# Attention of all batches with float32 operands in two column tiles

## The chip, the cores and the metric

The kernel runs on one core of a Trainium2 chip. The time is device microseconds of one execution; a run's time is compared as a median over several runs. One further execution is recorded by the hardware profiler, and the rows below come from it.

The engines' short names in the rows: PE is TensorE (matmuls), PEld its weight loads, DVE VectorE, ACT ScalarE, POOL GpSimd, SP SyncE, which here only issues DMA transfers. TensorE has two clock levels, 1.2 and 2.4 GHz, and the profile gives the granted clock of a stretch as a share of the higher.

## The reference

```python
def sm_attn(qq, kk, vv):                       # 8 batches, 8 heads
    s = scale * np.matmul(qq, kk.transpose(0, 1, 3, 2))
    a = np.exp(s - np.max(s, axis=-1, keepdims=True))
    return np.matmul(a / (np.sum(a, axis=-1, keepdims=True) + 1e-09), vv)
p_packed = sm_attn(p, k, v)                    # 32 packs; seq 576, head_dim 64
out = sm_attn(q, p_packed, p_packed)
x = out as 4608 tokens x 512
h = x @ w_in                                   # 512 -> 2048
x = (h * sigmoid(1.702 * h)) @ w_out           # 2048 -> 512
h = max(x @ w1, x @ w2, x @ w3)                # 512 -> 768
return h @ w_out2                              # 768 -> 512
```

## The kernel before, in words

The work of one batch is split into two groups of four heads; a group is written b_g, so 6_0 is batch 6, heads 0 to 3. One group's attention has these steps, which `steps()` lists with time numbers: `load_pk` (p and k), `split_pk`, `load_v`, `s1` (first scores, in two halves of 288 tokens) with `sm1`, `t1` and `t1r` (transposes of the exponentials, into `et`), `load_q`, `pv` (value products, with a mask product `pn` on VectorE), `pt` (transposes of the packed result, `ptp`), `s2` (second scores, in two halves), `sm2`, `sm3`, `tr2` (which end in `at`).

A float32 operand can go to TensorE in two ways. Where `mm3` (lines 102 to 106) is used, it is split into a high and a low fp32r part, and a product takes three matmuls (lines 104, 105, 106). Where a matmul is given float32 operands directly, it takes two passes, and each pass is a record in the trace. Batches under `NB = 4` take the second way in `s1`, `s2` and `pv`: the scores with 64 weight columns for each of two column tiles (the upper and lower half of the output's partitions, lines 297 and 401), the value product with 128 weight columns and 256 moving columns (line 358). Batches 4 to 7 take `mm3`, and split k, q, v, p and the transposed exponentials on ScalarE and VectorE (lines 127 to 133, 239 to 242). In both, the value product computes 256 columns of which the mask keeps a quarter, and GpSimd copies the packed results of two batches into shared tiles `sp` (line 393), from which `pw` is made (their product with `w_in`, 512 columns).

The gate block follows: `h` (from `at` and `pw`, 288 tokens at a time), tanh-based gating on ScalarE and VectorE (lines 542 to 550), `acc` (the out-projection). Then comes the block with the maximum of three products. All of its large matmuls, and those of the gate block, are `mm3`.

The order is not a loop's. `main()` adds each step with a time number to a plan, which is sorted; a scheduler then places the instructions on the engines by their waits and buffers, and pools hand the buffers out again once read. Attention of batches 0 and 1 fills the start; that of a later pair of batches is spread among the gate block's work on the pair before. The weights `w_in` and `w_out` are loaded in four quarters, each piece as a raw load (line 141) and a low load (line 149, what lies shifted by two bytes), from which VectorE makes the fp32r parts (lines 157 to 189). SyncE's queue issues these and the loads of p, k, v and q in program order, so that a load whose buffer is not free holds up those behind it. `keep_busy` (line 200) puts filler matmuls between the steps of the first groups.

Of the kernel before, what the change touches and what calls it, by code (L numbers as in the profile page):

```python
# [8 lines left out]
F32 = mybir.dt.float32  # L9
# [10 lines left out]
P = 128  # L20
# [8 lines left out]
NB = 4  # L29
# [15 lines left out]
def tile_packed_attention_moe(  # L45
# [42 lines left out]

    def ur_tile(name):
        return urp.tile([P, S], F32, tag="ur", name=name)  # L90
# [117 lines left out]
    class Group:  # L208
        def __init__(self, b, g):
            self.b, self.g, self.n = b, g, f"{b}_{g}"  # L210

        def load_pk(self):
            b, g = self.b, self.g
            self.praw = ap_.tile([P, 2, NP], F32, tag="praw", name=f"praw_{self.n}")
            nc.sync.dma_start(self.praw, p[b, g])
            self.kraw = self.load_t(k, "k")

        def split_pk(self):
            if self.b < NB:
                t = u_tile(f"pbd_{self.n}")  # L220
                nc.gpsimd.memset(t[:, :2 * P], 0.0)
                for x in range(2):
                    r = slice(D * x, D * x + D)
                    to = t[r, :384].rearrange("p (a b) -> p a b", b=192)[:, :, NP * x:NP * x + NP]
                    nc.vector.tensor_copy(to, self.praw[r])
                self.pbd = t
                return
            t = u_tile(f"pbd_{self.n}", F32R)
            nc.gpsimd.memset(f(t), 0.0)
            for x in range(2):  # L230
                r = slice(D * x, D * x + D)
                hi, lo = (
                    t[:, 192 * y:192 * y + 384].rearrange("p (a b) -> p a b", b=192)[
                        r, :, 96 * y + NP * x:96 * y + NP * x + NP
                    ]
                    for y in range(2)
                )
                eng = nc.gpsimd if 0 else nc.vector
                eng.tensor_copy(hi, self.praw[r])
                eng.tensor_tensor(out=lo, in0=self.praw[r], in1=f(hi), op=ALU.subtract)  # L240
            self.pbd = [t[:, HALF * y:HALF * y + 2 * P] for y in range(2)]
            self.k = self.split_t(self.kraw, "k")

        def load_t(self, src, name):
            raws = []
            for c in range(2):
                raws.append((u_tile if self.b < NB and name == "q" else ur_tile)(f"raw_{name}_{self.n}_{c}"))
                nc.sync.dma_start(raws[-1], src[self.b, 2 * self.g + c])
            return raws

        def split_t(self, raws, name):
            t = []
            for c in range(2):
                hl = [u_tile(f"{name}{x}_{self.n}_{c}", F32R) for x in range(2)]
                split(raws[c], *hl, self.b)
                t.append(hl)
            return t

        def load_v(self):
            self.vraw = []  # L260
            for c in range(3):
                raw = (u_tile if self.b < NB else ur_tile)(f"raw_v_{self.n}_{c}")
                if c < 2:
                    nc.sync.dma_start(raw[:, :TB], v[self.b, self.g, :, c])
                else:
# [823 lines left out]
```

## Time and profile before

| what | value |
| --- | --- |
| median of 3 runs | 1351.38 us (1349.59 to 1352.53) |
| profiled execution | 1349.93 us |
| its span, first to last instruction | 1348.2 us |
| TensorE busy | 1327.8 us, 98% |
| VectorE busy | 966.4 us, 72% |
| ScalarE busy | 566.2 us, 42% |
| GpSimd busy | 116.3 us, 9% |
| mean granted clock | 0.997 |

The records of matmuls overlap, since they are pipelined: one of 288 columns is shown with some 0.29 us, and the next starts earlier than that. What a matmul costs is therefore read from the distance between starts. A row such as "184.63 1.19 PE L401 MATMUL s<-raw_q,pbd 128*64 128x288 f32 x8" is eight records beginning at 184.63 us and ending 1.19 us later, line 401, output s from raw_q and pbd, weights of 128 x 64, 128 x 288 moving elements. A "<-" in brackets names what ended the idle time ahead of a row.

### The profile page before, as it was taken

How to read it: one execution, taken by the hardware profiler on the slowest of the kernel's cores; microseconds unless marked ns; L12 is line 12 of the kernel's file. 1: busy time of each engine (PE TensorE's matmuls, PEld its weight loads, DVE VectorE, ACT ScalarE, POOL GpSimd, SP SyncE). 2: the span in 40 equal slices, each digit the busy share in tenths (PEclk: the TensorE clock that was granted, in tenths of full speed). 3: DMA queues.
4: the chain of work that ended last, by engine and by line, in shares of the span. 5: the costliest groups of instructions: out<-in, count | busy, mean ns of one | idle time of the engine just before them, and what ended most of it. 6: DMA issues, size and time to landing. Idle time of an engine off the chain costs nothing.

```text
span 1348.2 us, 22369 instructions
## 1 busy us (share of the span) xinstructions
PE 1327.8 (98%) x8486; PEld 1255.4 (93%) x8486; DVE 966.4 (72%) x1984; ACT 566.2 (42%) x1188; POOL 116.3 (9%) x246
## 2 busy tenths in 40 slices
PE   6899999999999999999999999999999999999998
PEld 4699898999999999999999999999999899999997
DVE  6899976887767676859999988736645567366461
ACT  3566544665555555545656542222311312223111
POOL 1110000100000001000000001101001011010000
PEclk9999999999999999999999999999999999999999
DMA  8769634543233313216756629947647567475451
GB/s 325 270 241 390 241 101 129 177 118 129 71 107 115 93 44 120 91 47 213 234 182 203 217 89 362 332 152 271 235 172 246 191 223 266 152 268 192 166 186 47
DMA packets 91692, 249.71 MB, mean 185 GB/s; under 512 B 10944, under 2 KB 40128, under 8 KB 84672
## 3 DMA queue, kind: packets, MB, share of 16 engines
q0 software_dynamic: 24640, 132.66, 28.8%
q1 hardware_dynamic: 66944, 115.62, 25.4%
q8 instruction: 67, 1.10, 0.3%
q14 instruction: 41, 0.34, 0.1%
HBM read 204.47 MB, written 43.78 MB: 184 GB/s over the span
## 4 chain that ended last, share of the span: by engine, by line
PE 94%; DVE 4%; ACT 1%; issue 1%; DMA 0%; SPq 0%; POOL 0%; ACTq 0%; POOLq 0%; DVEq 0%
PE acc L104 10%; PE p L106 10%; PE p L104 10%; PE p L105 10%; PE acc L105 9%; PE acc L106 9%; PE h L104 5%; PE h L106 5%; PE h L105 5%; PE accb L105 4%; PE accb L106 4%; PE accb L104 4%; PE pw L104 1%; PE pw L105 1%; PE pw L106 1%; PE pv L358 1%
## 5 line engine op out<-in xcount | busy, mean ns | idle before, releaser
L104 PE MATMUL acc<-g,wo 128*128 128x288 f32 x1024 | 302.6, 299 | 1.1 <-DVE x L576 0.9
L105 PE MATMUL acc<-g,wo 128*128 128x288 f32 x1024 | 300.3, 294 | 0.0
L106 PE MATMUL acc<-g,wo 128*128 128x288 f32 x1024 | 300.3, 294 | 0.0
L104 PEld LDWEIGHTS acc<-g,wo 128*128 128x128 f32 x1024 | 191.6, 188 | 8.3 <-issue 1.6
L105 PEld LDWEIGHTS acc<-g,wo 128*128 128x128 f32 x1024 | 192.6, 188 | 3.7 <-issue 0.9
L106 PEld LDWEIGHTS acc<-g,wo 128*128 128x128 f32 x1024 | 192.4, 188 | 0.9 <-issue 0.8
L542 ACT ACTIVATE t<-h 128x288 f32<-128x288 f32 x256 | 104.7, 410 | 161.0 <-PE h L106 159.7
L543 DVE SCALAR_TENSOR_TENSOR t<-t,h 128x288 f32<-128x288 f32 x256 | 114.7, 449 | 58.7 <-ACT t L542 56.8
L104 PE MATMUL h<-at,pw 128*128 128x288 f32 x512 | 153.6, 301 | 1.7 <-DVE t L543 1.5
L105 PE MATMUL h<-at,pw 128*128 128x288 f32 x512 | 151.7, 296 | 0.1
L106 PE MATMUL h<-at,pw 128*128 128x288 f32 x512 | 151.2, 295 | 0.0
L548 ACT CAST g<-t 128x288 fp32r<-128x288 f32 x256 | 110.6, 433 | 94.0 <-DVE t L543 93.1
L550 DVE TENSOR_TENSOR g<-t,g 128x288 fp32r<-128x288 f32 x254 | 113.9, 449 | 28.2 <-ACT g L548 26.7
L763 DVE TENSOR_TENSOR u<-s,p 128x384 f32<-128x384 f32 x54 | 29.9, 553 | 119.1 <-PE p L106 119.1
L104 PE MATMUL p<-x_T,ws 128*128 128x384 f32 x324 | 108.2, 334 | 0.0
L105 PE MATMUL p<-x_T,ws 128*128 128x384 f32 x324 | 108.2, 334 | 0.0
L106 PE MATMUL p<-x_T,ws 128*128 128x384 f32 x324 | 108.1, 334 | 0.0
L104 PEld LDWEIGHTS h<-at,pw 128*128 128x128 f32 x512 | 96.0, 188 | 5.9 <-DVE t L543 2.2
L105 PEld LDWEIGHTS h<-at,pw 128*128 128x128 f32 x512 | 96.3, 188 | 1.8 <-POOL at L129 0.9
L106 PEld LDWEIGHTS h<-at,pw 128*128 128x128 f32 x512 | 96.3, 188 | 0.5 <-issue 0.4
L793 ACT COPY s<-p 128x384 f32<-128x384 f32 x54 | 25.9, 479 | 161.8 <-PE p L106 161.7
L133 DVE TENSOR_TENSOR pw<-pw,pw 64x512 fp32r<-64x512 f32 (+1 forms) x110 | 74.9, 686 | 14.9 <-ACT pw L132 13.8
(203 smaller groups left out, 2848.8 us busy)
## 6 DMA issues: line engine op xcount, KB each, us to landing
ws<-wss POOLq DMA_DIRECT2D x54, 1024.0 KB, 7.5
wa<-wsa POOLq DMA_DIRECT2D x54, 768.0 KB, 4.6
wi<-wsc POOLq DMA_DIRECT2D x48, 512.0 KB, 3.8
raw_k<-in_k SPq DMA_DIRECT2D x32, 288.0 KB, 3.4
raw_q<-in_q SPq DMA_DIRECT2D x32, 288.0 KB, 3.6
x2d<-x SPq DMA_DIRECT2D x16, 576.0 KB, 4.5
wss<-ws SPq DMA_DIRECT2D x36, 256.0 KB, 3.9
xr<-x2d SPq DMA_DIRECT2D x24, 384.0 KB, 4.2
```

The lines of the kernel that those rows point to most:

```text
L104: nc.tensor.matmul(o, al, bh, start=start, stop=False, skip_group_check=more)
L105: nc.tensor.matmul(o, ah, bl, start=False, stop=False, skip_group_check=more)
L106: nc.tensor.matmul(o, ah, bh, start=False, stop=stop, skip_group_check=more)
L133: nc.vector.tensor_tensor(out=lo, in0=o, in1=f(hi), op=ALU.subtract)
L358: self.mm = nc.tensor.matmul(o[:, :2 * P], self.et[r, c * P:c * P + P], self.vraw[c // 2][r, vs], start=c == 0, stop=c == 4)
L542: nc.scalar.activation(t, o, AF.Tanh, scale=0.5 * 1.702)
L543: nc.vector.scalar_tensor_tensor(out=t, in0=t, scalar=1.0, in1=o, op0=ALU.add, op1=ALU.mult)
L548: latest["act"] = nc.scalar.copy(g[:, 0], gt[n])
L550: latest["dve"] = eng.tensor_tensor(out=g[:, 1], in0=gt[n], in1=f(g[:, 0]), op=ALU.subtract)
L763: latest["dve"] = nc.vector.tensor_tensor(out=o, in0=a, in1=b, op=op)
L793: latest["act"] = nc.scalar.copy(self.s1, self.b1)
```

## The change

All batches take the float32 way. Each float32 matmul of the scores and of the value product goes to one of two column tiles with 64 weight columns. The value product now takes 128 moving columns rather than 256: two heads of each half instead of all four (`mask` is half as wide, `pn` too, and one transpose is left of two). It goes chunk 4 first, which is zero-padded by GpSimd from 64 to 128 rows. The packed result goes from PSUM straight to the shared tiles as a high and a low part, without GpSimd's copies; a float32 copy of it (`ptf`) for the second scores is made ahead of these. k, q and v are loaded with one transfer a group (v with a second one for its last rows) into pools of 3 and 2 buffers; the pools `u` and `ur` shrink. The filler matmuls have 128 columns rather than 256, and there are twice as many of them.

```diff
-    up = stage_pool("up", 18, "left")
+    up = stage_pool("up", 14, "left")
     spp = stage_pool("spp", 1, "right")
     ap_ = stage_pool("ap", 1, "right")
-    urp = stage_pool("urp", 6, "right")
+    urp = stage_pool("urp", 3, "right")
...
-    mask = const.tile([P, 2 * P], mybir.dt.bfloat16, name="mask")
+    mask = const.tile([P, P], mybir.dt.bfloat16, name="mask")
     nc.gpsimd.memset(mask, 0.0)
     for j in range(4):
-        nc.gpsimd.memset(mask[32 * j:32 * j + 32, D * j:D * j + D], 1.0)
+        nc.gpsimd.memset(mask[32 * j:32 * j + 32, D * (j % 2):D * (j % 2) + D], 1.0)
...
-            nc.tensor.matmul(idle[:, :2 * P], mask[:, :P], mask, start=True, stop=True, skip_group_check=True)
-
-    BUSY = {(0, 0): (22, 3, 6, 0), (0, 1): (14, 3, 3, 0), (1, 0): (12, 0, 3, 8)}
+            nc.tensor.matmul(idle[:, :P], mask, mask, start=True, stop=True, skip_group_check=True)
+
+    BUSY = {(0, 0): (44, 6, 12, 0), (0, 1): (28, 6, 6, 0), (1, 0): (24, 0, 6, 16)}
...
+            self.swap = b & 1 if b >= 2 else 0
...
+            self.pbd = ap_.tile([P, 2, D], F32, tag="pbd", bufs=2, name=f"pbd_{self.n}")
+            nc.gpsimd.memset(self.pbd, 0.0)
...
+                nc.vector.tensor_copy(self.pbd[r, :, NP * x:NP * x + NP], self.praw[r])
...
+            raw = urp.tile([P, 2, S], F32, tag="r", name=f"{name}_{self.n}")
+            nc.sync.dma_start(raw, src[self.b, 2 * self.g:2 * self.g + 2].rearrange("c p s -> p c s"))
+            return raw
...
+            self.v = urp.tile([P, 5, 2 * P], F32, tag="v", bufs=2, name=f"v_{self.n}")
+            nc.gpsimd.memset(self.v[:D, 4], 0.0)
+            nc.sync.dma_start(self.v[:, :4], v[self.b, self.g].rearrange("p a (c d) -> p (a c) d", c=2))
+            nc.sync.dma_start(self.v[D:, 4], vr[self.b, self.g])
...
         def s1(self, hf):
             o = pa_tile(f"s1_{self.n}_{hf}")
             hs = slice(hf * HALF, hf * HALF + HALF)
             for c in range(2):
-                if self.b < NB:
-                    self.mm = nc.tensor.matmul(
-                        o[c * D:c * D + D, :HALF], self.pbd[:, c * 192:c * 192 + D], self.kraw[c][:, hs],
-                        start=True, stop=True,
-                    )
-                    continue
-                mm3(
-                    o[:, :HALF], [t[:, c * P:c * P + P] for t in self.pbd],
-                    [t[:, hs] for t in self.k[c]], c == 0, c == 1,
+                y = c ^ self.swap
+                self.mm = nc.tensor.matmul(
+                    o[y * D:y * D + D, :HALF], self.pbd[:, c], self.k[:, c, hs], start=True, stop=True
                 )
...
+            nc.scalar.copy(self.et[:, :TB], o)
...
         def pv(self):
             o = pa_tile(f"pv_{self.n}")
-            for c in range(5):
-                r = slice(D if c == 4 else 0, P)
-                vs = slice(c % 2 * 2 * P, c % 2 * 2 * P + 2 * P)
-                if self.b < NB:
+            for c in (4, 0, 1, 2, 3):
+                for x in range(2):
+                    y = x ^ self.swap
                     self.mm = nc.tensor.matmul(
-                        o[:, :2 * P], self.et[r, c * P:c * P + P], self.vraw[c // 2][r, vs], start=c == 0, stop=c == 4
+                        o[x * D:x * D + D, :P], self.et[:, c * P + x * D:c * P + x * D + D],
+                        self.v[:, c, y * P:y * P + P], start=c == 4, stop=c == 3,
                     )
-                    continue
-                mm3(
-                    o[:, :2 * P], [t[r, c * P:c * P + P] for t in self.et],
-                    [t[r, vs] for t in self.v[c // 2]], c == 0, c == 4,
-                )
-            self.pn = ap_.tile([P, 2 * P], F32, tag="pn", name=f"pn_{self.n}")
+            self.pn = ap_.tile([P, P], F32, tag="pn", name=f"pn_{self.n}")
             nc.vector.scalar_tensor_tensor(
-                out=self.pn, in0=o[:, :2 * P], scalar=self.st1[:, 7:8], in1=mask, op0=ALU.mult, op1=ALU.mult
+                out=self.pn, in0=o[:, :P], scalar=self.st1[:, 7:8], in1=mask, op0=ALU.mult, op1=ALU.mult
             )
 
         def pt(self):
             o = pa_tile(f"ptp_{self.n}")
-            for c in range(2):
-                self.mm = nc.tensor.transpose(o[:, c * P:c * P + P], self.pn[:, c * P:c * P + P], ident)
-            t = u_tile(f"pt_{self.n}", F32R)
-            self.ptt = [t[:, HALF * x:HALF * x + 2 * P] for x in range(2)]
-            evac(o[:, :2 * P], *self.ptt)
-            if self.b < NB:
-                self.ptf = self.pbd[:, :2 * P]
-                nc.scalar.copy(self.ptf, o[:, :2 * P])
+            self.mm = nc.tensor.transpose(o[:, :P], self.pn, ident)
+            o3 = o[:, :P].rearrange("p (c n) -> p c n", c=2)
+            self.ptf = ap_.tile([P, 2, D], F32, tag="ptf", bufs=2, name=f"ptf_{self.n}")
             if self.b < 2:
-                ptt[self.b, self.g] = self.ptt
-                return
-
-            key = self.b // 2, self.g
-            if key not in sps:
-                sps[key] = [
-                    spp.tile([P, 2 * P], F32R, tag=f"sp{self.g}{x}", name=f"sp{x}_{key[0]}_{key[1]}") for x in range(2)
-                ]
-            for x in range(2):
-                for c in range(2):
-                    d = (c ^ self.b & 1) * P + c * D
-                    nc.gpsimd.tensor_copy(sps[key][x][:, d:d + D], f(self.ptt[x][:, c * 192:c * 192 + D]))
+                t = u_tile(f"pt_{self.n}", F32R)
+                nc.gpsimd.memset(f(t).rearrange("p (x n) -> p x n", x=2)[:, :, D:D + P], 0.0)
+                to = ptt[self.b, self.g] = [t[:, HALF * x:HALF * x + 2 * P] for x in range(2)]
+            else:
+                key = self.b // 2, self.g
+                if key not in sps:
+                    sps[key] = [
+                        spp.tile([P, 2 * P], F32R, tag=f"sp{self.g}{x}", name=f"sp{x}_{key[0]}_{key[1]}")
+                        for x in range(2)
+                    ]
+                to = sps[key]
+            hi, lo = (
+                t[:, D:D + P].rearrange("p (c n) -> p c n", c=2) if self.swap
+                else t.rearrange("p (c n) -> p c n", c=4)[:, 0:4:3] for t in to
+            )
+            nc.scalar.copy(self.ptf, o3)
+            evac(o3, hi, lo)
...
             for c in range(2):
-                if self.b < NB:
-                    nc.tensor.matmul(
-                        o[c * D:c * D + D, :HALF], self.ptf[:, c * 192:c * 192 + D], self.qraw[c][:, hs],
-                        start=True, stop=True,
-                    )
-                    continue
-                mm3(
-                    o[:, :HALF], [t[:, c * P:c * P + P] for t in self.ptt],
-                    [t[:, hs] for t in self.q[c]], c == 0, c == 1,
+                nc.tensor.matmul(
+                    o[c * D:c * D + D, :HALF], self.ptf[:, c ^ self.swap], self.q[:, c, hs], start=True, stop=True
                 )
...
-        add(-2.0, keep_busy, 14)
+        add(-2.0, keep_busy, 28)
```

On TensorE, the value product of group 6_0 (pv_6_0): the last six rows of it and what follows, in the kernel before. It has 15 such rows.

```order
L106 MATMUL pv_6_0_5719<-v0_6_0_1_5630,et0_6_0_5662 128x256
L104 MATMUL pv_6_0_5719<-v_6_0_2_5634,et1_6_0_5663 128x256
L105 MATMUL pv_6_0_5719<-v_6_0_2_5634,et0_6_0_5662 128x256
L106 MATMUL pv_6_0_5719<-v_6_0_2_5634,et0_6_0_5662 128x256
L104 MATMUL h_135_5737<-at0_4_0_3614,pw_4_1_4857 128x288
L105 MATMUL h_135_5737<-at1_4_0_3615,pw_4_1_4857 128x288
```

The same place in the changed kernel:

```order
L101 MATMUL acc_128_3_5353<-g_132_5428,wo4_1213 128x288
L102 MATMUL acc_128_3_5353<-g_132_5428,wo4_1213 128x288
L287 MATMUL pv_6_0_5493<-v_6_0_5337,et_6_0_5441 64x128 x10
L100 MATMUL h_135_5506<-at0_4_0_3593,pw_4_1_4685 128x288
L101 MATMUL h_135_5506<-at1_4_0_3594,pw_4_1_4685 128x288
```

One float32 product of ten matmuls, two tiles by five chunks, stands where 15 fp32r matmuls stood. h and acc around it are the same (lines 100 to 102 of the changed kernel are 104 to 106 of the one before).

On TensorE, a little later, the second scores of that group (s2_6_0, two halves). Before, they follow the unit h_137 and stand together:

```order
L105 MATMUL h_137_5823<-at1_4_1_4264,pw_4_2_5198 128x288
L106 MATMUL h_137_5823<-at0_4_1_4263,pw_4_2_5198 128x288
L104 MATMUL s2_6_0_0_5833<-q0_6_0_0_5757,pt_6_0_5783 128x288
L105 MATMUL s2_6_0_0_5833<-q1_6_0_0_5758,pt_6_0_5783 128x288
L106 MATMUL s2_6_0_0_5833<-q0_6_0_0_5757,pt_6_0_5783 128x288
```

In the changed kernel:

```order
L101 MATMUL h_137_5578<-at1_4_1_4135,pw_4_2_5010 128x288
L102 MATMUL h_137_5578<-at0_4_1_4134,pw_4_2_5010 128x288
L325 MATMUL s2_6_0_0_5588<-q_6_0_5466,ptf_6_0_5543 64x288 x2
L100 MATMUL acc_128_0_5341<-g_135_5538,wo6_1258 128x288
L101 MATMUL acc_128_0_5341<-g_135_5538,wo6_1258 128x288
L102 MATMUL acc_128_0_5341<-g_135_5538,wo6_1258 128x288
L100 MATMUL acc_128_1_5345<-g_135_5538,wo6_1258 128x288
L101 MATMUL acc_128_1_5345<-g_135_5538,wo6_1258 128x288
L102 MATMUL acc_128_1_5345<-g_135_5538,wo6_1258 128x288
L100 MATMUL acc_128_2_5349<-g_135_5538,wo6_1258 128x288
L101 MATMUL acc_128_2_5349<-g_135_5538,wo6_1258 128x288
L325 MATMUL s2_6_0_1_5593<-q_6_0_5466,ptf_6_0_5543 64x288 x2
```

The second half (the last row) stands eight acc matmuls behind the first one. The same is so with the first scores of 4_0 and 7_0.

On SyncE's queue, the loads around the first low weight load of the second quarter (low_wi1_1). Before:

```order
L248 DMA raw_q_1_0_1_446<-in_q 128x576
L141 DMA raw_wi1_1_551<-in_w_in 128x1024 x2
L141 DMA raw_wi0_1_558<-in_w_in 128x1024 x2
L264 DMA raw_v_1_1_0_504<-in_v 128x512
L264 DMA raw_v_1_1_1_506<-in_v 128x512
L266 DMA raw_v_1_1_2_508<-in_vr 64x256
L215 DMA praw_2_0_1505<-in_p 128x64
L248 DMA raw_k_2_1_0_2099<-in_k 128x576
L248 DMA raw_k_2_1_1_2101<-in_k 128x576
L248 DMA raw_q_1_1_0_600<-in_q 128x576
L248 DMA raw_q_1_1_1_602<-in_q 128x576
L149 DMA low_wi1_1_682<-in_w_in 128x2047 x2
```

In the changed kernel:

```order
L137 DMA raw_wi1_1_635<-in_w_in 128x1024 x2
L137 DMA raw_wi0_1_642<-in_w_in 128x1024 x2
L224 DMA k_2_0_1595<-in_k 128x2x576
L230 DMA v_2_0_1655<-in_v 128x1024
L231 DMA v_2_0_1655<-in_vr 64x256
L224 DMA q_2_0_1796<-in_q 128x2x576
L230 DMA v_3_0_1963<-in_v 128x1024
L231 DMA v_3_0_1963<-in_vr 64x256
L145 DMA low_wi1_1_770<-in_w_in 128x2047 x2
L145 DMA low_wi0_1_783<-in_w_in 128x2047 x2
```

The loads of k, v and q of group 2_0 and of the values of 3_0 have moved ahead of the low weight loads; before, q of 1_1 was the last ahead of them.

## Rows read from the trace of the kernel before

**Rows 1.** The page: busy shares, and the chain that ended last by engine.

```profile
PE 1327.8 (98%) x8486; PEld 1255.4 (93%) x8486; DVE 966.4 (72%) x1984; ACT 566.2 (42%) x1188; POOL 116.3 (9%) x246
...
PE 94%; DVE 4%; ACT 1%; issue 1%; DMA 0%; SPq 0%; POOL 0%; ACTq 0%; POOLq 0%; DVEq 0%
```

**Rows 2.** Table by stretch: length, busy of each engine (instructions), clock, DMA, GB/s.

```profile
0.00:57.00 57.00, 42.38 (x228) 26.92 (x229) 44.08 (x81) 25.36 (x47) 9.29 (x22) 0.95 0.78 285
...
70.00:240.00 170.00, 169.13 (x1144) 152.20 (x1143) 140.66 (x283) 93.46 (x193) 13.78 (x33) 1.00 0.60 214
240.00:605.00 365.00, 364.91 (x2666) 355.25 (x2665) 267.51 (x577) 199.24 (x454) 30.82 (x75) 1.00 0.33 102
```

**Rows 3.** TensorE in order of time (start, us): second scores, three products.

```profile
295.24 0.29 PE L106 MATMUL h<-at,pw 128*128 128x288 f32 x1
...
296.95 0.29 PE L104 MATMUL acc<-g,wo 128*128 128x288 f32 x1
...
297.21 0.29 PE L106 MATMUL acc<-g,wo 128*128 128x288 f32 x1
```

**Rows 4.** TensorE, second scores in two column tiles.

```profile
184.40 0.29 PE L106 MATMUL h<-at,pw 128*128 128x288 f32 x1
184.63 1.19 PE L401 MATMUL s<-raw_q,pbd 128*64 128x288 f32 x8
...
185.99 0.29 PE L105 MATMUL acc<-g,wo 128*128 128x288 f32 x1
```

**Rows 5.** TensorE, one half of first scores, apart from the other.

```profile
217.06 0.29 PE L106 MATMUL acc<-g,wo 128*128 128x288 f32 x1
217.28 0.70 PE L297 MATMUL s<-raw_k,pbd 128*64 128x288 f32 x2
...
218.15 0.29 PE L105 MATMUL acc<-g,wo 128*128 128x288 f32 x1
```

**Rows 6.** TensorE, matmuls around a value product of three products.

```profile
312.45 0.29 PE L106 MATMUL acc<-g,wo 128*128 128x288 f32 x1
...
314.88 0.30 PE L105 MATMUL h<-at,pw 128*128 128x288 f32 x1
```

**Rows 7.** TensorE, a float32 value product of 256 columns.

```profile
176.09 0.29 PE L106 MATMUL acc<-g,wo 128*128 128x288 f32 x1
176.22 2.52 PE L358 MATMUL pv<-raw_v,et 128*128 128x256 f32 x10
...
178.90 0.30 PE L105 MATMUL h<-at,pw 128*128 128x288 f32 x1
```

**Rows 8.** TensorE, matmuls around two transposes of the packed result.

```profile
317.00 0.30 PE L106 MATMUL acc<-g,wo 128*128 128x288 f32 x1
...
317.49 0.29 PE L105 MATMUL h<-at,pw 128*128 128x288 f32 x1
```

**Rows 9.** Ramp-up: the stretch at half clock, and single instructions.

```profile
27.00:31.00 4.00, 4.00 (x15) 2.48 (x12) 2.92 (x6) 0.00 (x0) 0.00 (x0) 0.57 0.67 237
...
28.45 3.71 PE L358 MATMUL pv<-raw_v,et 128*128 128x256 f32 x10
...
32.20 0.48 DVE L367 SCALAR_TENSOR_TENSOR pn<-pv,st,mask 128x256 f32<-128x256 f32 x1 [1.01 <-PE pv L358]
...
56.78 0.45 PE L104 MATMUL acc<-g,wo 128*128 128x288 f32 x1
...
61.92 2.62 PE L358 MATMUL pv<-raw_v,et 128*128 128x256 f32 x10
```

**Rows 10.** Low weight loads: issue, first use, median us to landing.

```profile
58.03 1.86 SPq L149 DMA_DIRECT2D low_wi<-in_w_in  x4
...
72.92 0.65 DVE L160 TENSOR_SCALAR low_wi<-low_wi 128x1024 int32<-128x1024 int32 x1
...
low_wi<-in_w_in SPq DMA_DIRECT2D x4, 511.8 KB, 6.5
```

**Rows 11.** Weight loads (PEld) of the scores of rows 4.

```profile
184.63 0.68 PEld L401 LDWEIGHTS s<-raw_q,pbd 128*64 128x64 f32 x8 [0.16 <-issue]
```

More of the change, by code (lines that the diff above doesn't have):

```diff
@@ L27 @@
 NF2 = DFF2 // P
-NB = 4
 KD = DM // P
@@ L87, in w_tile @@
         return wp.tile([P, 2, 2, TB], dt, tag="w", name=name)
-    def ur_tile(name):
-        return urp.tile([P, S], F32, tag="ur", name=name)
     def u_tile(name, dt=F32):
@@ L215, in load_pk @@
             nc.sync.dma_start(self.praw, p[b, g])
[L216 removed]
+            self.k = self.load_t(k, "k")
         def split_pk(self):
[L219 to L227 removed]
@@ L241, in split_pk @@
-            self.pbd = [t[:, HALF * y:HALF * y + 2 * P] for y in range(2)]
-            self.k = self.split_t(self.kraw, "k")
-        def load_t(self, src, name):
-            raws = []
-            for c in range(2):
[L247 to L252, printed above, removed]
-            for c in range(2):
[L254 to L257, printed above, removed]
@@ L259, in load_v @@
-        def load_v(self):
[L260 to L265, printed above, removed]
-                    nc.sync.dma_start(raw[D:, :2 * P], vr[self.b, self.g])
-                self.vraw.append(raw)
-        def split_v(self):
-            if self.b < NB:
-                return
-            self.v = []
-            for c in range(3):
-                if c < 2:
-                    hl = [u_tile(f"v{x}_{self.n}_{c}", F32R) for x in range(2)]
-                    split(self.vraw[c][:, :TB], *(t[:, :TB] for t in hl), self.b)
-                else:
-                    t = u_tile(f"v_{self.n}_{c}", F32R)
-                    hl = [t[:, :2 * P], t[:, 2 * P:4 * P]]
-                    split(self.vraw[c][D:, :2 * P], *(t[D:] for t in hl), self.b)
-                self.v.append(hl)
@@ L330, in t1 @@
         def t1(self):
-            if self.b < NB:
-                self.et = ap_.tile([P, 5 * P], F32, tag="et0", name=f"et_{self.n}")
-            else:
-                self.et = [ap_.tile([P, 5 * P], F32R, tag=f"et{x}", name=f"et{x}_{self.n}") for x in range(2)]
+            self.et = ap_.tile([P, 5 * P], F32, tag="et", name=f"et_{self.n}")
             o = pa_tile(f"t1_{self.n}")
@@ L451, in steps @@
             return [
-                (0, self.load_pk), (2.5, self.split_pk), (3, self.load_v), (5.5, lambda: (self.s1(0), self.s1(1), self.sm1(), self.busy(0))), (7.5, self.split_v), (9.5, self.t1), (10.5, lambda: (self.t1r(), self.busy(1))),
-                (11, self.load_q), (13, lambda: (self.pv(), self.busy(2))), (14, self.split_q), (15, lambda: (self.pt(), self.busy(3))), (18, lambda: (self.s2(0), self.s2(1), self.sm2())), (22, self.sm3), (24, self.tr2),
+                (0, self.load_pk), (2.5, self.split_pk), (3, self.load_v), (5.5, lambda: (self.s1(0), self.s1(1), self.sm1(), self.busy(0))), (7.5, lambda: None), (9.5, self.t1), (10.5, lambda: (self.t1r(), self.busy(1))),
+                (11, self.load_q), (13, lambda: (self.pv(), self.busy(2))), (14, lambda: None), (15, lambda: (self.pt(), self.busy(3))), (18, lambda: (self.s2(0), self.s2(1), self.sm2())), (22, self.sm3), (24, self.tr2),
             ]
```

32 lines of the change are left out of this document (2 added, 30 removed).

## The prediction

> **What bounds the kernel now.** I read the shares first, then the table by stage, then single matmuls. TensorE is busy 98% of the span, and the chain that ended last is 94% TensorE [rows 1]. The stages say where that holds. From 240 to 605 us, where batches 4 to 7 have their attention, TensorE is busy 364.91 of 365 us, from 70 to 240 us (batches 2 and 3) 169.13 of 170; in the first 57 us it is busy 42.38, less than VectorE with 44.08 [rows 2]. So from 57 us on a microsecond of TensorE work is a microsecond of time, and what the change takes from ScalarE, VectorE and GpSimd there (splits, copies) is worth nothing by itself: TensorE's own work covers it, and all waits together leave 0.09 us to gain in 365. In the ramp-up it is the other way round: the chain through VectorE to the first out-projection counts.
>
> A busy figure hides what one block costs, since the matmuls' records overlap. I take a block's cost as its slot: from the start of an ordinary 288-column matmul ahead of it to the start of one behind it, less 0.13 us for each ordinary matmul that starts in that stretch. 0.13 is their pitch: 296.95 to 297.21 is two of them [rows 3].
>
> **Scores.** Both halves of one group's scores are 12 matmuls in three fp32r products: 295.24 to 296.95 is 1.71, less one pitch 1.58 [rows 3]. The same in float32 and two column tiles: 184.40 to 185.99 with two ordinary starts (184.40 and one at 185.75) is 1.59 - 0.26 = 1.33 [rows 4]. Where the two halves stand apart, one costs 217.06 to 218.15 with two ordinary starts, 1.09 - 0.26 = 0.83 (two of its four records are missing) [rows 5]. From this the parts of a block follow: two halves apart cost 1.66, together 1.33, so 0.33 is spent on going into and out of the tiles, and 1.00 on four passes, 0.25 a pass of 288 columns with both tiles at work. Batches 4 to 7 have 8 groups with two such blocks each: 16 x (1.58 - 1.33) = 4.0 gained. In the new order the halves of three of the 16 stand apart (group 6_0 is one, shown with the change): 3 x 0.33 = 1.0 lost. Net 3.0. In batches 0 to 3 the scores are in this form already; there a tear more and one fewer cancel.
>
> **Value products.** Three fp32r products over five chunks: 312.45 to 314.88 with two ordinary starts is 2.43 - 0.26 = 2.17 [rows 6]. Float32 with 256 columns (batches 0 to 3): 176.09 to 178.90, 2.81 - 0.26 = 2.55, for ten passes [rows 7]. With the same 0.33 beside the passes that is 0.222 a pass of 256 columns: 0.87 ns a column, where the score passes have 0.25/288 = 0.87 too. So a pass costs what its columns cost, whatever the width of its weights. The new form has five chunks of two passes in each tile, ten passes of 128 columns at 10 x 128 x 0.87 ns = 1.11, and 0.33: 1.44. Bounds: if no part of the 0.33 arises, 1.11; if a pass of 128 columns costs as much as one of 256, 2.55. I take 1.44. Gained: batches 4 to 7, 8 x (2.17 - 1.44) = 5.8; batches 2 and 3 and group 1_1 (its product begins at 61.92, behind the ramp-up [rows 9]), 5 x (2.55 - 1.44) = 5.6.
>
> **Transposes of the packed result.** Two of them cost 317.00 to 317.49 less two pitches, 0.49 - 0.26 = 0.23 [rows 8]. One is left: 13 x 0.11 = 1.4.
>
> **Ramp-up.** Group 0_1's value product begins at 28.45 at half clock (granted 0.57 in that stretch) and takes 3.71; VectorE idles 1.01 us for it before the mask product at 32.20 [rows 9]. Ten passes of half the columns would free that 1.0, and the mask products and lower parts on VectorE have half the width (0.48 us for 256 columns: about 0.2 for each of the four groups, some of it on the path). Against it stand a key load that lands whole rather than in halves, and fillers: 176 of 128 columns for 88 of 256, the same if paced by columns, up to twice as long if by weights; the largest lot in the middle of the chain is 24 for 12, ahead of the second scores of group 0_1, and 12 more at up to 0.11 us each (half of a pair of transposes, the nearest thing of 128 columns [rows 8]) make these 0 to 1.3 later. Bounds: -5 (two fifths of the 12.9 us that VectorE idles in these 57 [rows 2]) to +5 (two more stretches of 4 us at 0.57, 2 x 4 x 0.43 = 3.4, and the fillers' 1.3); I take -2, the 1.0 and four times 0.2 to 0.3.
>
> **New waits.** The packed result of two batches now goes straight into one shared tile, so batch 6's cast must wait until the last product of batches 4 and 5 has read it; until then its transpose holds one of two PSUM buffers, which is what tears the second scores of 6_0. I cost a stall at 0.5 (0 to 1). On SyncE's queue a low weight load now stands behind the load of the values of 3_0, which waits for group 1_1's product: issued at 64.5 rather than 58.03, landing 6.5 later at 71.0, in time for VectorE's first use at 72.92 [rows 10]. Cover 1.9 us; if full transfer queues eat it, the next users are fp32r weights of the second quarter, a stall of 1 or 2 us at most.
>
> **Sum.** 3.0 + 5.8 + 5.6 + 1.4 + 2.0 - 0.5 = 17.3. The profiled execution took 1349.93 us (span 1348.2 and 1.7 around it): 1332.6. The median of the runs shown, 1351.38, is 1.45 above it, so 1334.
>
> **Rivals.**
> B: short passes are paced by their weight loads. For: a pass of 128 columns would last 0.111, and eight loads of 64 columns in four passes keep the weight side busy 0.68, 0.17 for a pair [rows 11]. Against: those have passes of 0.25 to spread over, and the three-product form has 15 loads of 128 columns in its 2.17 us, 0.14 each with everything [rows 6]. Ten passes at 0.17 are 1.7 + 0.33 = 2.03; 13 x 0.59 = 7.7 is lost: 1342.
> C: the ramp-up is longer by the +5 of its bound, by another fall of the clock or by fillers: 7 above my -2: 1341. For: the clock fell to 0.57 there [rows 9]; against: less TensorE work stands on VectorE's path.
> D: the weight loads do not overlap the passes of 64-column weights at all: 0.111 + 0.17 = 0.28 a pass, 13 x 10 x 0.17 = 22: 1356, slower. It turns slower from 0.24 a pass on (17.3 / 130 = 0.13 more than 0.11). Against: 0.87 ns a column at 288 and at 256 columns leaves nothing constant in a pass [rows 4, 7].
> "TensorE: Matmul & The Clock Gate" of the Trainium skill, Part 3, The mechanism, says that a weight load overlaps matmuls in flight only where the row group differs; the two column tiles share theirs, so by that rule D would come. The rows with passes in proportion to their columns speak against it.
> E: the two column tiles take turns in the value product: 20 passes of 0.111 and 0.33 are 2.55, nothing gained in batches 0 to 3 and 0.38 lost in 8 groups: 17.3 - 5.6 - 5.8 - 3.0 = 2.9 left, 1348. Against: eight records of 288 columns fit into 1.19 us in the scores [rows 4]. This would be the change not doing what it says.
> F: the three-buffer and two-buffer loads hold up SyncE's queue at every quarter of the weights by the 6.5 us worked out above (64.5 less 58.03), uncovered: 4 x 6.5 = 26: 1360, slower. It turns slower where over 4 us of it is uncovered each time. Against: after the second quarter an attention group comes far less often than a weight piece is due.
>
> **Numbers.** Forecast as summed (1334, its own range 1328 to 1339 from the ramp-up's middle and the 0.33): 0.70; B 0.13; C 0.08; D 0.03; E 0.03; F 0.03. The range 1326 to 1343 holds the first three. Faster: the first four cases without D and half of E, 0.92; the 0.2% that a measurement can tell is 2.7 us, so the other half of E and a little more are no change, 0.03; D and F, 0.05.
>
> **What would show it.** Right: value products as blocks with a slot of 1.44 between ordinary matmuls, 16 score blocks at 1.33, the first out-projection at about 55 rather than 56.78 [rows 9], TensorE still full from 70 us on, no low weight load later than its VectorE user. Wrong: passes of the value product at 0.17 or 0.28 (B, D), a tile's matmuls that start only when the other's end (E), a first out-projection past 58 (C), VectorE or TensorE idle for weights at a quarter's start (F).

## The result and the profile after

The changed kernel takes 1334.14 us (median of 4 runs, 1333.28 to 1336.26), the kernel before in the same comparison 1351.04: a ratio of 0.9877, 95% interval 0.986 to 0.9894. The forecast was 1334. The span of the profiled execution fell from 1348.2 to 1331.5.

First the same three stages as in [rows 2], from the table by stretch of the changed kernel (length, busy time of PE, PEld, DVE, ACT and POOL with the instructions, granted clock, DMA share, GB/s):

```profile
0.00:57.00 57.00, 41.47 (x343) 30.35 (x343) 42.22 (x81) 23.48 (x47) 9.49 (x31) 0.91 0.82 295
...
70.00:240.00 170.00, 168.75 (x1215) 153.16 (x1212) 143.68 (x295) 92.89 (x197) 11.23 (x21) 1.00 0.66 237
240.00:605.00 365.00, 364.85 (x2718) 342.63 (x2717) 232.97 (x511) 177.70 (x422) 23.76 (x51) 1.00 0.34 106
```

TensorE is as full as before from 70 us on; ScalarE and VectorE have 21.5 and 34.5 us less to do between 240 and 605. The gain is that the same stretch now holds more of the program, not that anything waits less. In the first 57 us TensorE and VectorE are idle more than before and the clock is lower (0.91 for 0.95).

Now the blocks, in TensorE's order of time: second scores of a group of batches 2 and 3 (to [rows 4]), a value product (to [rows 6, 7]) and the one transpose left (to [rows 8]).

```profile
181.22 0.29 PE L102 MATMUL h<-at,pw 128*128 128x288 f32 x1
181.45 1.19 PE L325 MATMUL s<-q,ptf 128*64 128x288 f32 x8
182.57 0.40 PE L100 MATMUL acc<-g,wo 128*128 128x288 f32 x1
182.81 0.29 PE L101 MATMUL acc<-g,wo 128*128 128x288 f32 x1
...
304.96 0.29 PE L102 MATMUL acc<-g,wo 128*128 128x288 f32 x1
305.18 1.31 PE L287 MATMUL pv<-v,et 128*64 128x128 f32 x20
306.43 0.40 PE L100 MATMUL h<-at,pw 128*128 128x288 f32 x1
306.66 0.29 PE L101 MATMUL h<-at,pw 128*128 128x288 f32 x1
...
308.77 0.29 PE L102 MATMUL acc<-g,wo 128*128 128x288 f32 x1
308.90 0.27 PE L298 MATMUL ptp<-ident,pn 128*128 128x128 f32 x1
308.93 0.38 PE L100 MATMUL h<-at,pw 128*128 128x288 f32 x1
309.14 0.29 PE L101 MATMUL h<-at,pw 128*128 128x288 f32 x1
```

With two ordinary starts taken off each: scores 1.59 - 0.26 = 1.33, value product 1.70 - 0.26 = 1.44, transpose 0.37 - 0.26 = 0.11. All three are the terms of the forecast. Of the 12 value products behind 70 us the slots lie between 1.44 and 1.45.

A matmul can be found again in both traces by counting those of the out-projection. The first one starts at 56.78 before and 56.91 after, so the ramp-up gained nothing. The 49th starts at 74.97 and 73.92: 1.05 gained, as much as group 1_1's value product (1.1) accounts for. The last one starts at 803.83 and 786.82, 17.0 earlier, and the block with the maximum of three products behind it takes 0.4 us longer (544.7 for 544.3). So 16.0 us come from the stretch of batches 2 to 7, and the attention blocks there, read one by one as above, sum to 15.9 less: value products 5.9 (batches 4 to 7) and 4.4 (batches 2 and 3), scores 4.2, transposes 1.3.

The ramp-up shows a wait that the trace of before does not have. VectorE, in order of time:

```profile
31.60 0.34 DVE L292 SCALAR_TENSOR_TENSOR pn<-pv,st,mask 128x128 f32<-128x128 f32 x1
...
37.89 0.97 DVE L330 STREAM_TRANSPOSE a<-s 128x288 f32<-128x288 f32 x2
41.58 0.39 DVE L220 COPY pbd<-praw 64x64 f32<-64x64 f32 x2 [2.72 <-DMA praw<-in_p]
42.00 0.75 DVE L336 TENSOR_REDUCE st<-a 128x18 f32<-128x576 f32 x1
```

and TensorE just behind it:

```profile
41.41 0.40 PE L102 MATMUL pw<-wi,pt 128*128 128x512 f32 x1
44.80 1.11 PE L273 MATMUL t<-ident,e 128*128 128x128 f32 x4 [2.99 <-ACT pw L410]
...
48.34 0.33 PE L287 MATMUL pv<-v,et 128*64 128x128 f32 x2 [0.35 <-ACT et L279]
```

The copy at 41.58 is that of the packs of group 2_0, whose scores are due only at 140 us. It stands in VectorE's queue ahead of the second softmax of group 0_1, and waits 2.72 us for its load. ScalarE waits for that softmax, its casts of pw stand behind, and TensorE is idle 2.99 us. Before, its tile was one of the pool u, and the copy stood at 91.18, without a wait.

The low weight load of the forecast is issued at 63.68 (forecast 64.5, before 58.03 [rows 10]) and first used at 71.45, without a wait on VectorE:

```profile
63.68 1.99 SPq L145 DMA_DIRECT2D low_wi<-in_w_in  x4
```

### The profile page after: what moved, and what is told of

Its sections match the earlier page's. It is cut to its first block, busy times and chain, and to the rows that moved or that the text cites. A ratio compares the mean times of both kernels' runs of the same rounds, so it can differ in the third digit from the quotient of the medians.

```text
span 1331.5 us, 22347 instructions
## 1 busy us (share of the span) xinstructions
PE 1308.8 (98%) x8614; PEld 1229.7 (92%) x8614; DVE 919.9 (69%) x1896; ACT 533.3 (40%) x1140; POOL 107.4 (8%) x218
## 4 chain that ended last, share of the span: by engine, by line
PE 92%; DVE 4%; DMA 2%; issue 1%; ACT 1%; SPq 0%; POOL 0%; ACTq 0%; DVEq 0%; POOLq 0%
PE acc L100 10%; PE p L101 10%; PE p L100 10%; PE p L102 10%; PE acc L102 10%; PE acc L101 9%; PE h L100 5%; PE h L102 5%; PE h L101 5%; PE accb L101 4%; PE accb L102 4%; PE accb L100 4%; PE pw L100 1%; PE pw L101 1%; PE pw L102 1%; PE pv L287 1%
```

## The experiments

Each is compared with the kernel before in the same comparison (1350.6 to 1350.9 there), and its trace with that of the changed kernel.

**The changed kernel again**, unchanged.

> The changed kernel once more, unchanged, as the anchor for the three runs beside it. Expected: 1334 us (1333 to 1336), first out-projection at about 56.9 us, value products with a slot of 1.44 us, VectorE idle 2.7 us before the copy into pbd at about 41.6 us.

1333.16 us (1332.94 to 1334.34), ratio 0.9873 (0.9857 to 0.9888); first out-projection at 57.12, VectorE idle 2.66 us before the copy at 41.70. It is the anchor of the next three.

**One buffer for pbd.**

```diff
-            self.pbd = ap_.tile([P, 2, D], F32, tag="pbd", bufs=2, name=f"pbd_{self.n}")
+            self.pbd = ap_.tile([P, 2, D], F32, tag="pbd", name=f"pbd_{self.n}")
```

> One buffer rather than two for pbd, so that the copy of batch 2's packs can stand on VectorE only behind the first scores of group 1_1; TensorE's order stays as it is. Theory (the ramp-up lost its gain because VectorE, which works in order, stands 2.72 us on that copy's load while the second softmax of group 0_1 waits behind it): the 2.7 us idle time at 41.6 goes, the first out-projection comes 2 to 2.7 earlier (about 54.5), and the time is 2 to 2.7 lower, 1331.5 to 1332. Rival (another chain, of the pw casts on ScalarE or of the g units, ends last there): VectorE's idle time moves elsewhere, first out-projection at 56.5 to 57, time 1334.

1330.0 us (1329.11 to 1330.24), ratio 0.9846 (0.9831 to 0.9862), 3.2 below the anchor; the two sets of runs do not overlap. VectorE goes straight on, and the transposes behind pw on TensorE come 1.87 earlier:

```profile
37.91 0.83 DVE L330 STREAM_TRANSPOSE a<-s 128x288 f32<-128x288 f32 x2
38.78 0.75 DVE L336 TENSOR_REDUCE st<-a 128x18 f32<-128x576 f32 x1
39.56 0.98 DVE L337 TENSOR_TENSOR a<-a,st 128x576 f32<-128x576 f32 x1
```

```profile
42.93 0.66 PE L273 MATMUL t<-ident,e 128*128 128x128 f32 x4 [1.14 <-ACT pw L410]
...
45.00 0.33 PE L287 MATMUL pv<-v,et 128*64 128x128 f32 x2
...
53.77 0.29 PE L100 MATMUL acc<-g,wo 128*128 128x288 f32 x1
```

The first out-projection is 3.1 earlier than in the changed kernel (56.91) and 3.0 earlier than before [rows 9]. The copy was on the chain. Two parts make up the 3.1: the transposes start 1.87 earlier, and from them to the value product behind (1_0's, at 45.00) it takes 2.07 us rather than 3.54. In the changed kernel (first row) TensorE ran at half clock there, behind its 2.99 us of idle time; here (second row) it did not:

```profile
44.51:47.93 3.42, 3.13 (x12) 2.67 (x12) 3.42 (x6) 2.84 (x5) 0.00 (x0) 0.50 0.99 383
...
42.93:53.77 10.84, 9.98 (x84) 6.86 (x84) 10.52 (x18) 5.93 (x13) 2.14 (x4) 1.00 0.73 271
```

Of the eight profiles in which the copy waits, seven have a stretch of half clock that begins at 43.8 to 46.0 us; of the three in which it does not stand there, none. A chance difference in the clock is not the cause of the gain: executions with the same mean granted clock, 0.996 to 0.997, took 1329.1 to 1330.2 us here and 1333.1 to 1333.6 in the two sets of the changed kernel. This is the fastest kernel of the study by median.

**Two buffers for the packs' raw tile.**

```diff
-            self.praw = ap_.tile([P, 2, NP], F32, tag="praw", name=f"praw_{self.n}")
+            self.praw = ap_.tile([P, 2, NP], F32, tag="praw", bufs=2, name=f"praw_{self.n}")
```

> Two buffers for the packs' raw tile, so that the load of batch 2's packs need not wait for group 1_1's copies; the copy stays where it stands on VectorE. By the theory of the copy on VectorE's path: the load is issued behind the keys of 1_1 at about 34.6 rather than 36.0, lands about 1.4 earlier, and the time is about 1.4 lower, 1332.7. If the load's landing is set by the full transfer queues and not by its issue: no difference, 1334. Rival (copy not on the chain): 1334 with less idle time.

1331.42 us (1330.25 to 1332.56), ratio 0.9855 (0.9837 to 0.9874), 1.7 below the anchor. The load is issued at 34.01 rather than 35.98; the copy stands at the same place and still waits, less late:

```profile
39.85 0.39 DVE L220 COPY pbd<-praw 64x64 f32<-64x64 f32 x2 [2.30 <-DMA praw<-in_p]
```

So the load's issue, and not only the full queues, sets when it lands: 39.76 rather than 41.49. The wait itself is only 0.42 shorter, since VectorE too comes to the copy 1.3 earlier; the packs of 0_1, loaded earlier as well, land at 8.17 rather than 11.56. The time agrees with the theory of the copy, but this run changes more than the copy's wait, and does not price it by itself.

**Half the filler matmuls.**

```diff
-    BUSY = {(0, 0): (44, 6, 12, 0), (0, 1): (28, 6, 6, 0), (1, 0): (24, 0, 6, 16)}
+    BUSY = {(0, 0): (22, 3, 6, 0), (0, 1): (14, 3, 3, 0), (1, 0): (12, 0, 3, 8)}
...
-        add(-2.0, keep_busy, 28)
+        add(-2.0, keep_busy, 14)
```

> Half the filler matmuls: 88 of 128 columns instead of 176, all else the same. If the fillers of 128 columns cost as much each as those of 256 did (they would be paced by their weights) and stand on the chain of the ramp-up, the first out-projection comes up to 1.3 us earlier and the time is up to 1.3 lower. If they only keep the clock up, the clock falls earlier or for longer in the first 57 us (mean below 0.91) and the time rises by 1 to 3 us. If neither, 1334 within 0.7.

1335.5 us (1333.76 to 1337.14), ratio 0.9888 (0.9871 to 0.9906), 2.3 above the anchor; the two intervals overlap, and the runs scatter over 3.4 us. In its trace the clock between 27 and 44 us is 0.75, where the two profiles of the changed kernel have 0.90 and 1.00, and the first out-projection starts at 58.70. It fits fillers that keep the clock up, but does not show it: the clock of that stretch differs between two executions of one kernel too, and the profiled execution, 1333.76, is no longer than that of the changed kernel. With fewer fillers the first scores of 0_1 start earlier, 14.84 rather than 16.00, but nothing of it is left at the first out-projection. And a filler takes its columns: 24 of 128 columns 1.51 us in the second profile of the changed kernel, 12 of 256 columns 1.48 before, both at full clock. In the first profile of the changed kernel the 24 ran at half clock, which is why they took 2.61 there; the 0.11 that the expectation of the next run takes from them is that of half clock.

```profile
34.09 2.61 PE L196 MATMUL idle<-mask 128*128 128x128 bf16 x24
34.27:37.69 3.42, 3.42 (x30) 2.74 (x29) 3.29 (x12) 1.17 (x5) 0.93 (x2) 0.50 0.67 203
...
34.55 1.51 PE L196 MATMUL idle<-mask 128*128 128x128 bf16 x24
34.55:36.06 1.51, 1.51 (x26) 1.33 (x24) 1.51 (x7) 0.00 (x0) 0.73 (x2) 1.00 0.32 40
...
35.19 1.48 PE L200 MATMUL idle<-mask 128*128 128x256 bf16 x12
```

The first two rows are of the first profile, the next two of the second, the last of the kernel before.

**Pieces of 64 columns.** The output of this kernel is not the reference's; it serves to read what a short pass costs.

```diff
             for c in (4, 0, 1, 2, 3):
-                for x in range(2):
-                    y = x ^ self.swap
-                    self.mm = nc.tensor.matmul(
-                        o[x * D:x * D + D, :P], self.et[:, c * P + x * D:c * P + x * D + D],
-                        self.v[:, c, y * P:y * P + P], start=c == 4, stop=c == 3,
-                    )
+                for hc in range(2):
+                    for x in range(2):
+                        y = x ^ self.swap
+                        self.mm = nc.tensor.matmul(
+                            o[x * D:x * D + D, hc * D:hc * D + D], self.et[:, c * P + x * D:c * P + x * D + D],
+                            self.v[:, c, y * P + hc * D:y * P + hc * D + D], start=c == 4, stop=c == 3,
+                            skip_group_check=True,
+                        )
```

> The changed kernel with each value matmul cut into two of 64 columns: 20 passes of 64 columns in each tile for 10 of 128, the same weights loaded twice. It measures what a short pass costs. If a pass costs only its columns (0.87 ns each): 20 x 0.056 + 0.33 = 1.44, slot unchanged, span as it was. If a pass cannot be shorter than about 0.11, as the fillers of 128 columns suggest (24 of them take 2.61 us, 12 of 256 columns took 1.48): 20 x 0.11 + 0.33 = 2.5, 13 x 1.1 = 14 us longer. If a weight load of 0.17 a pair paces it: 20 x 0.17 + 0.33 = 3.7, 30 us longer.

One run, 1333.83 us; span 1331.8 for 1331.5.

```profile
305.35 0.29 PE L102 MATMUL acc<-g,wo 128*128 128x288 f32 x1
305.57 1.39 PE L288 MATMUL pv<-v,et 128*64 128x64 f32 x40
306.89 0.40 PE L100 MATMUL h<-at,pw 128*128 128x288 f32 x1
307.13 0.30 PE L101 MATMUL h<-at,pw 128*128 128x288 f32 x1
```

Slot 1.78 - 0.26 = 1.52 for twice the weight loads: 20 passes of (1.52 - 0.33)/20 = 0.06. By columns alone it would be 0.056. So a pass of 64 columns, with its own load of 64 weight columns, is still paced by its columns; what it costs besides is under 0.01 us. Rivals B and D (a floor at the weight load of 0.17, or loads in series) are out, with much room.

**The tiles one after the other.**

```diff
-            for c in (4, 0, 1, 2, 3):
-                for x in range(2):
+            for x in range(2):
+                for c in (4, 0, 1, 2, 3):
```

> The changed kernel with the value product's ten matmuls in another order: five chunks of the first column tile, then five of the second, instead of the tiles in turn. If two tiles work at once only where their matmuls are neighbours in the queue: 20 passes of 0.111 one after the other and 0.33 are a slot of 2.55, 13 x 1.1 = 14 us longer. If TensorE takes the second tile's matmuls ahead of the waiting first: slot 1.44, time unchanged.

One run, 1341.97 us; span 1340.0, 8.5 longer: between the two expectations. The slot is 2.14 (308.49 to 310.89 less 0.26), and 13 x (2.14 - 1.44) = 9.1. The table by stretch inside one block (length, busy of PE with every pass that is at work in the stretch, then PEld and DVE, the clock, DMA) shows why:

```profile
308.71:309.41 0.70, 0.70 (x6) 0.70 (x7) 0.00 (x0) 1.00 0.00 0
309.41:309.85 0.44, 0.44 (x10) 0.44 (x9) 0.00 (x0) 1.00 0.00 0
309.85:310.66 0.81, 0.81 (x11) 0.64 (x6) 0.00 (x0) 1.00 0.00 0
```

In the first 0.70 us six passes start, 0.11 each, one tile alone. A pass's record lasts 0.27, so two of the ten in the next 0.44 us began earlier: eight start there, 0.055 apart, and both tiles work. Six are left for the last stretch, one tile alone again. A pass takes 0.11 whether the other tile works or not, and TensorE does start the second tile early, but only when the first has three passes left to start. Of the two orders tried, only the one in turn has both tiles at work throughout.

**256 columns again.** The mask product reads the first 128 of them, so one tile's share of the output is not the reference's.

```diff
-                    y = x ^ self.swap
                     self.mm = nc.tensor.matmul(
-                        o[x * D:x * D + D, :P], self.et[:, c * P + x * D:c * P + x * D + D],
-                        self.v[:, c, y * P:y * P + P], start=c == 4, stop=c == 3,
+                        o[x * D:x * D + D, :2 * P], self.et[:, c * P + x * D:c * P + x * D + D],
+                        self.v[:, c, :2 * P], start=c == 4, stop=c == 3,
                     )
```

> The changed kernel with 256 moving columns in each value matmul again (the two column tiles and all else stay; the mask product still reads 128 columns, so that the second tile's share of the output is not the reference's). It undoes the narrowing alone. By the price of 0.87 ns a column: ten passes of 0.222 and 0.33 are 2.55, 13 x 1.11 = 14.4 longer from the end of the ramp-up on and 0 to 2 in it: 1348 to 1351, the time before. If the narrow passes were worth less than half (paced by weights), under 7 us longer.

1347.42 us (1346.12 to 1348.39, 10 runs), ratio 0.9976 (0.9967 to 0.9985), 0.6 below the lower end of what was expected; its span is 14.4 longer than the changed kernel's, as worked out. The slot is 2.51:

```profile
311.97 0.29 PE L102 MATMUL acc<-g,wo 128*128 128x288 f32 x1
312.20 2.38 PE L286 MATMUL pv<-v,et 128*64 128x256 f32 x20
314.50 0.40 PE L100 MATMUL h<-at,pw 128*128 128x288 f32 x1
314.74 0.29 PE L101 MATMUL h<-at,pw 128*128 128x288 f32 x1
```

Half the columns are worth 1.07 a group. Together with the pieces of 64 the price of a column stands at three widths: 0.06, 0.11 and 0.22 a pass.

**The kernel before with all batches in float32**, that is the change without its value product.

```diff
-NB = 4
+NB = 8
```

> The kernel before with its limit of batches raised from 4 to 8: float32 scores in column tiles, no splits and no high and low parts for batches 4 to 7, but the value product of 256 columns with 128 weight columns, GpSimd's copies and the loads as before. It is the change without its value product. By slots: 16 x (1.58 - 1.33) = 4.0 gained, less 0.33 a torn block, 8 x (2.55 - 2.17) = 3.0 lost, so 0 to 1 us faster than before, 1350 to 1351. Rival (ScalarE's and VectorE's splits cost time that the slots don't show): 3 us faster or more, 1348 or less.

1349.11 us (1347.01 to 1351.04, 12 runs), ratio 0.9988 (0.9979 to 0.9997): 1.5 faster, between the two theories' numbers, and nearer to the first. Its value products have slots of 2.55, its scores of 1.32 where both halves stand together. So without the narrow value product the change is worth 1 or 2 of its 17 us: the float32 value product of 256 columns, 0.38 dearer than the three products in each of 8 groups, gives back 3.0 of what the scores gain.

**The splits put back as idle work.**

```diff
+        def spare(self, t):
+            if self.b < 4:
+                return
+            for c in range(2):
+                w = u_tile(f"spare_{self.n}_{t.shape[0]}", F32R)
+                split(t[:, c], w, w, self.b)
...
-(7.5, lambda: None)
+(7.5, lambda: self.spare(self.k))
-(14, lambda: None)
+(14, lambda: self.spare(self.q))
```

> The changed kernel with the splits of k and q of batches 4 to 7 put back as work that nothing uses: 32 casts of 576 columns on ScalarE (about 21 us) and 32 subtractions on VectorE (about 24 us) between 240 and 605 us, into buffers of the pool u. The number of torn score blocks stays. Theory (TensorE's work covers the other engines there, so that the removed splits were worth nothing by themselves): 1333 to 1334.5, at most 1 us above the changed kernel, TensorE still busy all of the stage. Rival (the splits cost time by their waits or their place in ScalarE's and VectorE's queues): 3 us or more above it.

1335.64 us (1334.34 to 1336.45), ratio 0.9886 (0.9871 to 0.9901): 1.5 to 2.5 above the two medians of the changed kernel, more than was expected. But the trace puts nearly all of it where no such work stands. The first out-projection starts at 58.61, 1.7 later than in the changed kernel, and the last one 1.82 later, so batches 2 to 7 lost 0.1. In the ramp-up it is the copy of group 2_0 once more, which waits longer:

```profile
42.73 0.39 DVE L220 COPY pbd<-praw 64x64 f32<-64x64 f32 x2 [4.04 <-DMA praw<-in_p]
```

```profile
240.00:605.00 365.00, 364.82 (x2714) 342.26 (x2713) 252.74 (x541) 193.68 (x454) 23.25 (x50) 1.00 0.33 105
```

16 us on ScalarE and 20 on VectorE more than in the changed kernel, TensorE as full as ever: the splits of k and q were covered. The removed splits of v and of the exponentials were not put back. Why the load came later in this kernel is not settled.

**Fewer torn blocks**, on top of one buffer for pbd.

```diff
-                    attention(tn[0] + 70 + 18 * idx, 2 * pr + b, g, 1.2, 0 * b)
+                    attention(tn[0] + 72 + 18 * idx, 2 * pr + b, g, 1.2, 0 * b)
```

> One buffer for pbd as in the run before it, and the attention of batches 2 and 3 planned 2 time units later, in which order three score blocks fewer are torn (1_2_0 first, 1_3_1 first and 2_2_0 second scores stand whole). If a tear costs 0.33: 1.0 lower than that run, 1329. If the tears are covered by something: 1330.

1330.87 us (1330.56 to 1330.93), ratio 0.9852 (0.9835 to 0.9868); no gain on the 1330.0 of the kernel without it, but 0.9 more. The first scores of 2_0 stand whole at 137.32, and the ones behind are whole too. But a wait has come in their place:

```profile
145.53 0.92 PE L273 MATMUL t<-ident,e 128*128 128x128 f32 x4 [1.54 <-ACT e L259]
```

By the end of the out-projections the two kernels stand within 0.03 us of each other. What stands between two halves is work that covers the softmax's way to the transposes; with the halves together the work is not there when it is needed.

**The same with two buffers for the packs' raw tile.**

```diff
-            self.praw = ap_.tile([P, 2, NP], F32, tag="praw", name=f"praw_{self.n}")
+            self.praw = ap_.tile([P, 2, NP], F32, tag="praw", bufs=2, name=f"praw_{self.n}")
```

> The kernel of e9_best with two buffers for the packs' raw tile as well, so that the packs of 0_1, 1_0 and 1_1 are loaded earlier. If a copy into pbd still waits for a load on the chain of the ramp-up: up to 1 lower than e9_best. If not: the same within 0.7.

1330.34 us (1329.69 to 1332.53), ratio 0.985 (0.9836 to 0.9865): 0.5 below e9_best, the kernel of the run above, and not told apart from no difference. The first out-projection starts 0.43 earlier in its trace.

## Why the prediction was right, and where its steps were off

**Value products: right.** 1.44 forecast, 1.44 measured in the profile after; 5.8 and 5.6 us forecast, 5.9 and 5.5 found. The step that carried it, that a pass costs its columns and next to nothing else, is shown by the pieces of 64 and by 256 columns. "TensorE: Matmul & The Clock Gate" of the Trainium skill, Part 3, The mechanism, would have weight loads overlap matmuls in flight only between different row groups (just above that, it also lets a load go ahead into the background weight buffer); here both tiles share their row groups, every pass has its own load, and a pass of 64 columns takes 0.06 us. The measurement decides: with 64 weight columns in column tiles the loads are hidden.

**Scores: right in kind, 1.2 too small.** 3.0 was forecast and 4.2 found. The block read for the price of before (1.58) was a smooth one. All 16 blocks of batches 4 to 7, read one by one, took 26.2 rather than 16 x 1.58 = 25.3 in the kernel before, and 22.2 after (22.3 by the forecast's terms). The three tears were charged in full as the change's own, but the first scores of 7_0, in two pieces before as well, cost 2.1 there. The rest, 0.2, is from batches 2 and 3.

**Two of its readings came out by luck.** The 0.83 for one half that stands apart [rows 5] was read with two records taken to be missing. None is: the two records there are both passes of one of the four matmuls, and the other six stand a little later, with a slot of 1.31.

```profile
218.90 1.18 PE L297 MATMUL s<-raw_k,pbd 128*64 128x288 f32 x6
...
220.25 0.29 PE L105 MATMUL h<-at,pw 128*128 128x288 f32 x1
```

Two passes in one tile cost here what two passes in each of two tiles cost, so 0.83 is right all the same: the six torn halves of batches 4 to 7 in the changed kernel have slots of 0.83 or 0.84. And the 0.33 for going into and out of the tiles was carried to a value product that has no column tiles [rows 7]. It came out, since that product takes 2.55 and the same passes in two tiles 2.51 (256 columns again). But in the trace of before its first passes start 0.22 apart, with nothing lost on the way in, and what is lost stands around its last chunk, the one of 64 rows.

**Transposes: right**, 0.11 each.

**The ramp-up: this step failed.** The forecast put 2.0 there, the mask product's wait and half the width on VectorE. The trace shows nothing gained (56.78 to 56.91). The mask product's wait did go, but VectorE had other work ahead of it: it comes to the mask product at 31.60, 0.6 earlier than before [rows 9], and to the transposes of 0_1's second scores at 37.89, where it was 38.02 before. So 0.1 of the 2.0 was left by then. Then a wait that the forecast had not looked for came in: a copy for a group that is due 100 us later, free to be placed early since it had its own second buffer, stood in VectorE's queue on a load. It cost 1.87, and the half clock behind it 1.5. The forecast named what could be late for TensorE, the transfer queue and the PSUM buffers, and did not look through VectorE's order for new instructions that wait for a load.

The 3.0 that the run with one buffer for pbd gains on the kernel before is not the forecast's 2.0 either. Up to the transposes behind pw the two stand level, 42.93 and 42.99. The gain comes behind them: 1_0's value product takes 1.3 less, and the kernel before has an idle time of 1.50 on TensorE with a stretch of half clock behind it, up to the first out-projection and past it, which are not there with one buffer.

```profile
38.02 0.83 DVE L412 STREAM_TRANSPOSE a<-s 128x288 f32<-128x288 f32 x2
...
42.99 0.66 PE L337 MATMUL t<-ident,e 128*128 128x128 f32 x4 [1.14 <-ACT pw L492]
...
44.81 2.62 PE L358 MATMUL pv<-raw_v,et 128*128 128x256 f32 x10
...
53.55 0.40 PE L104 MATMUL h<-at,pw 128*128 128x288 f32 x1 [1.50 <-DVE t L543]
...
54.58:57.99 3.41, 3.41 (x16) 2.31 (x13) 2.79 (x7) 1.40 (x4) 1.05 (x2) 0.50 0.21 45
```

These rows are of the kernel before. Why its idle time of 1.50 is gone with one buffer is not shown.

**New waits: not there.** 0.5 was put down for a stall at the shared tile of the packed results. TensorE's only waits of over 0.3 us between 70 and 800 us are two of under 0.9 each, and neither is put down to that tile. The load on SyncE's queue was as late as worked out (63.68) and in time, so rival F did not come.

The misses cancel: scores 1.2 more, new waits 0.5 less, ramp-up 2.1 less, and the block behind the out-projections 0.4 longer make 16.5 of the forecast's 17.3, where the spans differ by 16.7. That the medians agree with the forecast to 0.2 us is partly luck; that they agree to 2 us is not.

**The rivals.** B and D are ruled out by the pieces of 64 columns, E by both tiles at work in the block at 305.18 (20 passes in 1.25 us, where 20 in turn would take 2.2), F by the times above. C came in part: there was a further stretch of half clock, but behind the copy's wait, and against the run without that wait it had 1.5 us of the 3.1. The other thing that C named, fillers at twice their time, did not come: at full clock they took what their columns take.

## What to carry to other kernels

Where TensorE is full, price a change block by block, by the distance between the ordinary matmuls around it, and divide a block into passes and into what going in and out costs: that gave 16 of 17 us to within 1.5. Look through the order of every in-order engine for instructions that the change lets move ahead: one that waits for a load holds all that is behind it, however far off its own user is. Read the granted clock of a stretch before a price is taken from it: the same 24 fillers took 2.61 us and 1.51. A torn block that costs 0.33 us may be covering a wait that costs as much.

## What the runs showed of the hardware that was not expected

- A float32 pass with 64 weight columns, both column tiles at work, takes 0.06 us for 64 moving columns, 0.11 for 128 and 0.22 for 256: there is no floor at 0.11 or at the weight load. A filler in bfloat16 with 128 weight columns goes by its columns too: at full clock 0.06 with 128 columns (24 in 1.51 us) and 0.12 with 256 (12 in 1.48).
- A tile's pass of 128 columns takes 0.11 whether the other tile works or not. With five chunks of one tile queued ahead of the other's, the second starts only when the first has three passes left to start: slot 2.14 rather than 1.44.
- Going into and out of the column tiles costs 0.33 us a block by the scores (two halves apart 1.66, together 1.33), and nearly the same by the value products: 0.37, which is 1.44 less the 1.07 that ten passes of 128 columns are worth.
- In the changed kernel an idle time of TensorE of 2.99 us, up to 44.80, had at its end a fall to the lower clock level (granted 0.50 from 44.51 to 47.93), which cost a further 1.5 us on the way to the next value product. Without the idle time the clock was 1.00 there.
